# Convolution windows of three quarters with their own halo rows, and chunks that enter in pairs

## The chip, the cores and the metric

The kernel runs on one core of one Trainium2 chip. The metric is device time in microseconds, a median over runs. A profile of one execution gives the busy times of TensorE (PE), its weight loads (PEld), VectorE (DVE), ScalarE (ACT), GpSimd (POOL) and the DMA queues, among them SyncE's (SP).

## The reference

A causal convolution over 7 tokens, one softmaxed set of taps per head of 24 channels, is followed by a token mix over all 4224 tokens and a channel mix:

```python
w = softmax(weight, axis=-1)                   # 8 heads x 7 taps
x = conv(x, w)                                 # x: 8 x 4224 x 192, left padding of 6 zeros
theta = x @ w_theta
zr, zi = x * cos(theta), x * sin(theta)
y = w_tok_r @ zr + w_tok_i @ zi                # 4224 x 4224 each, over tokens
u = x + y
out = u + max(u @ w_ch, 0)
```

## The kernel before, in words

**Tiling.** Batch and channels lie side by side: a token is a row of 1536 values. The 4224 tokens that are summed over are cut into 33 *chunks* of 128 rows; a chunk is four *quarters* of 32 tokens that lie far apart (`tokens(c, a)`, line 158), so that 32x32 transposes can turn the token weights. The 4224 tokens that are put out are cut into 16 *units* of two 128-row tiles and one unit of a single tile. For a unit of two tiles a fast matrix product with seven products takes the place of eight; each product is done for two halves g of 384 columns. So a unit costs 14 matmuls of 384 columns per chunk (8 for the single tile).

**Chunks and visits.** At most `SLOTS` = 11 chunks lie in SBUF as operands (tiles r0, i0, r1, i1, t1, t2, t4). `FIRST` says in which visit of the first round each of the first 11 chunks enters; later chunks enter 17 visits after the chunk whose slot they take (lines 109 to 111). A *visit* is one unit against the chunks that are in: it loads its sums d from DRAM (L621), transposes the token weights (L507) and adds and subtracts them (L521), runs the products (L659), adds the results to d (L686 on DVE; the first of a unit's first visit are ACT copies, L684), and stores d (L698). L731 copies a partial product from bank x to bank y. In the first round visit v has v + 1 chunks, up to 11; there are 61 visits. A unit's last visit ends with the channel mix: ACT casts d (L780), a transpose by DMA or, in the last four visits, by TensorE (L438, copied by DVE in L443), the mix (L452), the final add (L799) and the store (L806).

**Preparing a chunk** (`Chunk.prepare`). POOL loads the four quarters of x with a cast (L224, 32 rows each). The tile xw holds two halves of 96 rows: two quarters with 16 halo rows each. The halo comes from the chunk before by a DMA from SBUF to SBUF on SP's queue (L265, four per chunk). Two matmuls per head accumulate the two halves (L403, 96 rows by 192 columns, 16 per chunk); the weights are banded matrices made at the start (L826 to L875). ACT copies two heads at a time to xz (L411, four per chunk). SP stores xz (L298) for the later residual. xz is transposed, by TensorE for the first 11 chunks and by DMA after, mixed with theta's weights (L452), clamped by DVE (L320), turned to sine and cosine by ACT (L348), multiplied (L357) and subtracted (L369). xw and xz have two buffers each.

**Order.** Every piece of work is a `Step` with an engine, a planned duration and what it must follow. `Schedule` plays the steps through a model of the engines, takes the ready step with the earliest due time, and emits the instructions in that order; a rehearsal sets the due times. Each engine then runs its instructions strictly in that order. Constants such as `LAND` (planned DMA times) and `START` (when each engine is through with the preamble) belong to this model. Banks 0 to 5 of PSUM hold the products (rows x, y, s for two g); only banks 6 and 7 serve convolution, transposes and mixes: a step with `mm` takes one, and the step with `frees` gives it back.

Of the kernel before, what the change touches and what calls it, by code (L numbers as in the profile page):

```python
# [16 lines left out]
def kernel(  # L17
# [22 lines left out]
    nc = tc.nc  # L40
# [9 lines left out]
    HALO = 16  # L50
    WR = Q + HALO
    NT = S // P
    HN = N // 2
# [4 lines left out]
    FIRST = (0, 1, 2, 3, 4, 5, 6, 7, 8, 9, 10)  # L58
    CLAMP = 1.5
    EXTRA = 3  # L60
    BY_PE = 4
    SMALL = 3
# [73 lines left out]
    def pair(u):  # L136
        return 2 * u + 1 < NT


    def pair(u):  # L140
        return 2 * u + 1 < NT


# [22 lines left out]
    class Step:  # L166
        def __init__(self, engine, us, run, after=(), lands=0.0, wire=0.0, frees=None, mm=False):
            self.engine, self.us, self.run = engine, us, run
            self.after, self.lands, self.wire = list(after), lands, wire
            self.frees, self.mm = frees, mm  # L170
            self.due, self.want, self.fixed, self.end = None, None, None, None
            self.number = len(steps)
            steps.append(self)

# [20 lines left out]

    bands = constp.tile([2 * WR, 2 * H + 1, 2, Q], BF16, name="bands")
    nc.vector.memset(bands, 0.0)


    def channel_weights(w, name, after=()):  # L200
        R = D - P
        made = {}

        def clear():
            made["t"] = t = wk.tile([P, 4, D], BF16, name=name, tag="wc", bufs=1)
            dve(nc.vector.memset(t[:, 1:3, :], 0.0))

        ready = [Step("dve", 0.25, clear, after)]
        for lo, hi, k, r0, r1 in ((0, P, 0, 0, P), (0, R, 1, P, D), (R, P, 2, 0, R), (0, P, 3, R, D)):
            ready.append(Step(  # L210
                "pool", 0.6, lambda lo=lo, hi=hi, k=k, r0=r0, r1=r1: pool(nc.gpsimd.dma_start(
                    out=made["t"][lo:hi, k, :], in_=w[r0:r1, :]
                )), ready[:1], lands=4.0, wire=0.3,
            ))
        return (lambda: made["t"]), ready

    xw = tiles(wk, 2, [2 * WR, 2, B, D], BF16, "xw")
    rings = {k: Ring(2) for k in ("xw", "xz", "uT", "ang", "xr", "st", "x", "y", "s")}
# [4 lines left out]
    def load_x(c, a, n, lo, t0, h, k):  # L223
        pool(nc.gpsimd.dma_start(  # L224
            out=xw[k][lo : lo + n, h, :, :],
            in_=x[:, t0 : t0 + n, :].rearrange("b s d -> s b d"),
        ))


    class Chunk:  # L230
        def __init__(self, c):
            self.c, self.early = c, c < SLOTS
            self.k, self.uses, prev = rings["xw"].take()
            self.loads = []
            for a in range(NQ):
                h, lo = a // 2, (a % 2) * WR
                t0 = tokens(c, a)
                if c or t0 == 0:
                    lo += HALO
                else:  # L240
                    t0 -= HALO
                n = (a % 2 + 1) * WR - lo
                args = (c, a, n, lo, t0, h, self.k)
                if c == 0:
                    if t0 == 0:
                        nc.vector.memset(xw[0][0:HALO, 0, :, :], 0.0)
                    load_x(*args)
                    s = Step("none", 0.0, None)
                    s.fixed = START["x0"]
                else:  # L250
                    s = Step(
                        "pool", 0.6, lambda args=args: load_x(*args), [prev],
                        lands=LAND["x"], wire=0.87,
                    )
                self.loads.append(s)
            self.uses += self.loads
            chunks[c] = self
            xwk = xw[self.k]
            self.filled = list(self.loads)
            if c:  # L260
                before = chunks[c - 1]

                def history(a):
                    h, lo = a // 2, (a % 2) * WR
                    sp(nc.sync.dma_start(  # L265
                        out=xwk[lo : lo + HALO, h, :, :],
                        in_=xw[before.k][lo + Q : lo + Q + HALO, h, :, :],
                    ))

                for a in range(NQ):  # L270
                    s = Step(
                        "sp", 0.6, lambda a=a: history(a), [before.loads, prev],
                        lands=LAND["history"], wire=0.15,
                    )
                    before.uses.append(s)
                    self.filled.append(s)
            self.uses += self.filled[NQ:]

        def prepare(self):
            c = self.c  # L280
            zk, self.xzuse, prev = rings["xz"].take()
            self.xz = xzt[zk]
            copies = []
            for hp in range(H // 2):
                m = Step("pe", 0.34, lambda b, hp=hp: self.conv(b, hp), [self.filled, bands_ready, prev], mm=True)
                self.uses.append(m)
                e = Step(
                    "act", 0.5, lambda b, hp=hp: self.conv_copy(b, hp), [m], frees=m
                )
                copies.append(e)  # L290
            self.xzuse += copies
            self.xf = self.xz[:, :, :].rearrange("p b d -> p (b d)")
            if c + 2 < NCH:
                Chunk(c + 2)
# [8 lines left out]
            for g in range(2):  # L303
# [3 lines left out]
                turned = transposed(src, uT, [copies, prev], self.early, "sp")  # L307
# [4 lines left out]
                for k2 in range(2):  # L312
# [3 lines left out]
                    )  # L316
                    uuse.append(m)
# [80 lines left out]
        def conv(self, b, hp):  # L398
            for hh in range(2):
                h = 2 * hp + hh  # L400
                for half in range(2):
                    at = 2 * h + 1 - half
                    pe(nc.tensor.matmul(  # L403
                        banks[b][:, hh * B * G : (hh + 1) * B * G],
                        lhsT=bands[:, at : at + 2, :, :].rearrange("p z a m -> p (z a m)"),
                        rhs=xw[self.k][:, half, :, h * G : (h + 1) * G],
                        start=(half == 0), stop=(half == 1),
                    ))

        def conv_copy(self, b, hp):  # L410
            act(nc.scalar.activation(  # L411
                out=self.xz[:, :, hp * 2 * G : (hp + 1) * 2 * G].rearrange(
                    "p b (h g) -> p h b g", h=2
                ),
                in_=banks[b][:, 0 : 2 * B * G].rearrange("p (h b g) -> p h b g", h=2, b=B),
                func=AT.Copy,
            ))

# [7 lines left out]
    def transposed(u, uT, after, by_pe, queue):  # L426
# [8 lines left out]
        def turn(b):  # L435
# [7 lines left out]
        e = Step("dve", 0.55, lambda b: dve(nc.vector.tensor_copy(  # L443
            out=got(uT).rearrange("p k s -> p (k s)"),
            in_=banks[b][:, :].bitcast(BF16)[:, 0 : 6 * P],
        )), [m], frees=m)
# [19 lines left out]
    class Weights:  # L466
# [89 lines left out]
        def tile(self, name):  # L556
            t = self.tiles[name]
            return small_tile()[:, t] if self.small else t
# [7 lines left out]
    def freed_xw():  # L566
        return [s for u in rings["xw"].uses[-2:] for s in u]


    def small_tile():  # L570
        big_tile()
        if "small" not in late:
            late["small"] = wk.tile([P, 7, SMALL, NQ, Q], BF16, name="small", tag="xw")
        return late["small"]

    def big_tile():
        if "big" not in late:
            late["big"] = wk.tile([P, 2, HN], F32, name="late", tag="xw")
        return late["big"]
# [5 lines left out]
    def container(k):  # L585
        if ("u", k) not in late:
            if k < 4:
                both = wk.tile([P, 2, HN], BF16, name="ubT", tag=("ang", "xz")[k % 2])
# [10 lines left out]
    class Visit:  # L599
# [79 lines left out]
        def add(self, q, bank, g, after, begins=False, ends=False):  # L679
            def run():  # L680
                o = self.d[q]()[:, g * PC : (g + 1) * PC]
                y = banks[bank][:, 0:PC]
                if self.first and begins:
                    act(nc.scalar.activation(out=o, in_=y, func=AT.Copy))  # L684
                else:
                    dve(nc.vector.tensor_tensor(out=o, in0=y, in1=o, op=ALU.add))  # L686

            if self.first and begins:
                s = Step("act", 0.49, run, [after, self.start[q]])
# [14 lines left out]
        def products(self):  # L704
# [4 lines left out]
            for r in "xys" if self.pair else "xy":  # L709
                for g in gs:  # L710
                    k, uses[r, g], prev[r, g] = rings[r].take()
                    rows[r, g] = 2 * "xys".index(r) + k

# [15 lines left out]
            def copy(g):  # L729
                kx, ky = rows["x", g], rows["y", g]  # L730
                s = Step("act", 0.48, lambda: act(nc.scalar.activation(  # L731
                    out=banks[ky][:, 0:PC], in_=banks[kx][:, 0:PC], func=AT.Copy
                )), [at["x", g], prev["y", g]])
# [39 lines left out]
        def output(self, q):  # L773
            k, use, prev = outring.take()
            if len(outring.uses) <= 5:
                prev = [
                    s for r in ("ang", "xz", "uT") for u in rings[r].uses[-2:] for s in u
# [37 lines left out]
    START = {"x0": 8.0, "pe": 12.3, "dve": 12.3, "act": 6.3, "pool": 6.6, "sp": 2.0}  # L815
    LAND = {
        "x": 9.0, "history": 6.0, "keep": 6.0, "turn": 11.0, "w": 8.0, "d": 7.5, "store": 5.5,
        "xr": 7.0, "out": 5.0,
    }
    EARLY, SLACK = {}, 12.0  # L820
    noise = wk.tile([P, 512], BF16, name="noise", tag="ang")
    nc.vector.memset(noise, 0.0)
    Chunk(0)
    masks = wk.tile([2 * WR, KS, 2, Q], BF16, name="masks", tag="ang")
# [240 lines left out]
```

## Time and profile before

| what | value |
|---|---|
| three runs | 1449.01, 1450.27, 1439.24 us; median 1449.01 |
| profiled execution | 1439.62 us, span 1437.5 us, mean granted clock 0.997 |
| PE busy | 1408.2 us, 98% of the span, 9486 matmuls |
| DVE / ACT / POOL busy | 1102.9 / 335.8 / 512.2 us |
| L659, products | 7656 matmuls (7572 from tile w, 84 from tile small) |
| L403, convolution | 528 matmuls |
| L411, copies of the convolution | 132, 489 ns each, on ACT |
| L224, loads of x | 132 |
| L265, halo copies by DMA | 128 |
| L443, copies of transposes | 38, 549 ns each, on DVE |

A line of the groups reads: line, engine, operation, output<-input, shape, count, then busy time and mean duration, then the idle time of the engine just before these instructions and what ended it. Matmuls overlap in the array, so that a matmul's duration is longer than its distance from the next.

### The profile page before, as it was taken

What the parts mean: (1) busy time and instruction counts of PE and PEld (TensorE: products, weight loads), DVE (VectorE), ACT (ScalarE), POOL (GpSimd) and SP (SyncE); (2) the same over time, 40 slices, a digit from 0 to 9 for tenths busy, and PEclk for the clock granted to TensorE, in tenths of its full rate; (3) what the DMA queues carried; (4) which work ended last, traced back from release to release, by engine and by line L of the source; (5) the groups of instructions that cost most, each with busy time, mean ns of one, the idle gap of its engine ahead of it and who ended that gap; (6) DMA issues with size and microseconds to landing.
All of it is one profiled execution on the core that took longest, in us unless ns stands there. A gap on an engine that the chain in (4) does not pass through costs nothing.

```text
span 1437.5 us, 24960 instructions
## 1 busy us (share of the span) xinstructions
PE 1408.2 (98%) x9486; PEld 895.5 (62%) x9486; DVE 1102.9 (77%) x1835; ACT 335.8 (23%) x582; POOL 512.2 (36%) x778
## 2 busy tenths in 40 slices
PE   6899999999999999999999999999999999999997
PEld 3666666666666666666666666666666666666665
DVE  7998764446778887886576788788887878787788
ACT  5764422122212212210000221122121212121221
POOL 7543321124234552133134445225553354311120
PEclk9999999999999999999999999999999999999999
DMA  9999883679999999998799999999995999999984
GB/s 140 252 220 209 155 162 94 122 131 238 202 222 239 237 225 229 225 210 198 183 195 193 234 252 234 220 224 217 250 253 124 204 279 257 220 229 208 254 209 154
DMA packets 341351, 298.44 MB, mean 208 GB/s; under 512 B 160784, under 2 KB 287760, under 8 KB 341232
## 3 DMA queue, kind: packets, MB, share of 16 engines
q0 software_dynamic: 171072, 97.81, 50.5%
q1 hardware_dynamic: 130160, 189.21, 42.6%
q10 hardware_dynamic: 40000, 9.84, 5.3%
q8 instruction: 74, 1.21, 0.4%
q14 instruction: 45, 0.37, 0.1%
HBM read 250.21 MB, written 106.56 MB: 248 GB/s over the span
## 4 chain that ended last, share of the span: by engine, by line
PE 90%; DMA 4%; DVE 2%; ACT 1%; issue 0%; ACTq 0%; DVEq 0%
PE bank L659 82%; PE bank L452 5%; DMA ubT<-ubT 3%; PE bank L403 3%; DMA out_dram<-d 1%; PE bank L438 1%; DVE d L799 0%; DVE d L686 0%; DVE w L521 0%; DMA xw<-xw 0%; DVE ubT L443 0%; ACT ubT L780 0%; DVE uT L443 0%; ACT bank L731 0%; DVE ang L320 0%
## 5 line engine op out<-in xcount | busy, mean ns | idle before, releaser
L659 PEld LDWEIGHTS <-w 128*128 128x128 bf16 x7572 | 736.7, 98 | 466.5 <-issue 5.1
L659 PE MATMUL bank<-t,w 128*128 128x384 bf16 x3198 | 558.4, 326 | 1.6 <-DVE w L521 1.4
L686 DVE TENSOR_TENSOR d<-bank,d 128x384 f32<-128x384 f32 x542 | 291.8, 548 | 186.0 <-PE bank L659 158.0
L659 PE MATMUL bank<-i,w 128*128 128x384 bf16 x2220 | 396.2, 326 | 1.2 <-ACT bank L731 0.6
L507 DVE STREAM_TRANSPOSE w<-st 128x640 bf16<-128x640 bf16 (+5 forms) x416 | 340.2, 846 | 67.0 <-PE bank L659 63.0
L659 PE MATMUL bank<-r,w 128*128 128x384 bf16 x2154 | 384.1, 326 | 1.4 <-DVE r L357 1.2
L485 POOL DMA_DIRECT2D st<-in_moe_w_tok_r_dram x244 | 140.2, 585 | 411.4 <-DVE w L507 354.5
L485 POOL DMA_DIRECT2D st<-in_moe_w_tok_i_dram x244 | 139.8, 583 | 145.8 <-DVE w L507 138.8
L521 DVE TENSOR_TENSOR w<-w 128x1408 bf16<-128x1408 bf16 (+10 forms) x220 | 183.2, 833 | 2.5
L631 POOL TENSOR_TENSOR d<-d,xr 128x768 f32<-128x768 f32 x62 | 105.6, 1704 | 142.1 <-DMA xr<-xs 91.8
L224 POOL DMA_DIRECT2D xw<-in_x_dram x132 | 76.8, 594 | 153.6 <-PE bank L403 128.0
L348 ACT ACTIVATE r<-ang,half_pi 128x768 bf16<-128x768 f32 x44 | 41.1, 933 | 310.3 <-DVE ang L320 310.3
L731 ACT ACTIVATE bank<-bank 128x384 f32<-128x384 f32 x116 | 54.8, 476 | 211.8 <-PE bank L659 196.7
L684 ACT ACTIVATE d<-bank 128x384 f32<-128x384 f32 x132 | 63.4, 491 | 160.4 <-PE bank L659 158.8
L411 ACT ACTIVATE xz<-bank 128x384 bf16<-128x384 f32 x132 | 60.5, 489 | 168.8 <-issue 115.4
L320 DVE TENSOR_SCALAR ang<-bank 128x384 f32<-128x384 f32 x132 | 68.5, 550 | 24.8 <-PE bank L452 24.4
L780 ACT ACTIVATE ubT<-d 128x768 bf16<-128x768 f32 x44 | 36.8, 842 | 147.1 <-DVE d L686 116.3
L799 DVE SCALAR_TENSOR_TENSOR d<-bank,d 128x384 f32<-128x384 f32 x106 | 55.3, 550 | 20.7 <-PE bank L452 20.1
L452 PEld LDWEIGHTS <-uT 128*128 128x128 bf16 x632 | 55.0, 98 | 17.0 <-issue 3.0
L403 PE MATMUL bank<-xw,bands 96*128 96x192 bf16 x528 | 60.6, 249 | 1.9 <-ACT xz L411 1.1
L452 PE MATMUL bank<-wth,uT 128*128 128x192 bf16 x528 | 58.0, 246 | 2.6 <-DVE ang L320 1.1
L403 PEld LDWEIGHTS <-bands 96*128 96x128 bf16 x528 | 47.4, 99 | 15.3 <-issue 4.0
(68 smaller groups left out, 546.3 us busy)
## 6 DMA issues: line engine op xcount, KB each, us to landing
part<-d SPq DMA_DIRECT2D x172, 384.0 KB, 4.2
d<-part SPq DMA_DIRECT2D x159, 384.0 KB, 5.5
st<-in_moe_w_tok_r_dram POOLq DMA_DIRECT2D x152, 176.0 KB, 6.5
st<-in_moe_w_tok_i_dram POOLq DMA_DIRECT2D x152, 176.0 KB, 7.4
out_dram<-d SPq DMA_DIRECT2D x53, 384.0 KB, 5.8
xs<-xz SPq DMA_DIRECT2D x132, 96.0 KB, 5.0
xr<-xs POOLq DMA_DIRECT2D x66, 192.0 KB, 6.4
xw<-in_x_dram POOLq DMA_DIRECT2D x129, 96.0 KB, 5.7
```

What stands on the lines that cost most here:

```text
L224: pool(nc.gpsimd.dma_start(out=xw[k][lo : lo + n, h, :, :], in_=x[:, t0 : t0 + n, :].rearrange("b s d -> s b d"),))
L320: "dve", 0.55, lambda b, k2=k2, g=g: dve(nc.vector.tensor_scalar(out=self.ang[g][:, k2 * 2 * D : (k2 + 1) * 2 * D], in0=banks[b][:, 0 : 2 ...
L403: pe(nc.tensor.matmul(banks[b][:, hh * B * G : (hh + 1) * B * G], lhsT=bands[:, at : at + 2, :, :].rearrange("p z a m -> p (z a m)"), rhs= ...
L411: act(nc.scalar.activation(out=self.xz[:, :, hp * 2 * G : (hp + 1) * 2 * G].rearrange("p b (h g) -> p h b g", h=2), in_=banks[b][:, 0 : 2 ...
L452: pe(nc.tensor.matmul(banks[bk][:, b * D : (b + 1) * D], lhsT=tT[:, 3 * k + b + i, :], rhs=w[:, 2 * b + i, :], start=(i == 0), stop=(i == ...
L485: "pool", 0.58, lambda a=a, t0=t0, i=i, w=w: pool(nc.gpsimd.dma_start(out=st[i][a * Q : (a + 1) * Q, 0:nb, 0 : n * Q], in_=w[r0 : r0 + nb ...
L507: lambda c=c, ce=ce: dve(nc.vector.transpose(self.tile(name)[:, c:ce, :, :], st[i][:, at : at + NQ, c * Q : ce * Q].rearrange("p bt (c j) ...
L521: s = Step("dve", 0.15 + 0.069 * n, lambda: dve(nc.vector.tensor_tensor(out=flat(self.tile(name)), in0=flat(self.tile(p)), in1=flat(self.t ...
L631: a = Step("pool", 1.75, lambda: pool(nc.gpsimd.tensor_tensor(out=tile_(), in0=tile_(), in1=xrt[k], op=ALU.add)), [r, s])
L659: pe(nc.tensor.matmul(banks[bank][:, 0:PC], lhsT=self.w.block(a, c), rhs=chunks[c].operand(b, g), start=(start and c == self.lo), stop=(c ...
L684: act(nc.scalar.activation(out=o, in_=y, func=AT.Copy))
L686: dve(nc.vector.tensor_tensor(out=o, in0=y, in1=o, op=ALU.add))
```

## The change

- `FIRST` becomes (0, 0, 1, 2, 3, 4, 5, 6, 7, 8, 8): the first two and the last two chunks of a round enter together. The first round starts with two chunks; chunks also enter in pairs at visits 17, 25, 34 and 42. There are 59 visits, and two small visits are moved forward in place of three.
- A *window* of three quarters takes the place of the chunk as the unit of the convolution: 3 x 38 = 114 rows, each quarter with its own 6 halo rows, loaded from DRAM. The halo copies on SP go away. One matmul per head and window does three quarters; 44 windows. The band tile has seven quarter blocks with the fourth zero, so that a slice of four blocks puts the three results on the right output rows, whichever quarter the window begins with.
- A window that spans two chunks, or begins with an odd quarter, needs two copies out of the bank: 28 copies per three chunks. `readers` counts them; the bank is free after the last.
- xw and xz have three buffers each; late tiles that reuse this space are cut to match.
- *Copies on either engine* (`copy_step`, `also`): the planner gives them to ACT or DVE, whichever takes them first: convolution copies of chunks under 4, first copies of a visit and bank copies in visits under 4, and all copies of TensorE's transposes. Other such copies stay on ACT.
- *Lent banks*: until the first visit's products need them, banks 2 to 5 serve the convolution of windows 0 and 1 and the transposes and mixes of chunk 0 (`lent`). The first visit's y rows begin with a matmul whose result is overwritten.
- The preamble makes the band tile in one product and three halving adds; warm-up matmuls are 24, not 18, and need only the zeroed noise tile; theta's weights and the first two windows are loaded by the preamble itself.

```diff
-    FIRST = (0, 1, 2, 3, 4, 5, 6, 7, 8, 9, 10)
+    FIRST = (0, 0, 1, 2, 3, 4, 5, 6, 7, 8, 8)
+    EITHER, TURNED = 4, 11
...
+    def copy_step(o, i, after, us, frees=None, either=False):
+        def run(*b):
+            if s.engine == "dve":
+                dve(nc.vector.tensor_copy(out=o(), in_=i(*b)))
+            else:
+                act(nc.scalar.activation(out=o(), in_=i(*b), func=AT.Copy))
+        s = Step("act", us, run, after, frees=frees)
+        s.also = "dve" if either else None
+        return s
...
-    bands = constp.tile([2 * WR, 2 * H + 1, 2, Q], BF16, name="bands")
-    nc.vector.memset(bands, 0.0)
+    bands = constp.tile([WR, H, NQ + WQ, Q], BF16, name="bands")
+    nc.vector.memset(bands[:, :, WQ, :], 0.0)
...
+    class Window:
+            for j in range(WQ):
+                c, a = divmod(self.m * WQ + j, NQ)
+                lo, t0, n = j * ROWS, tokens(c, a) - KS + 1, ROWS
...
+                def load(lo=lo, t0=t0, n=n):
+                    pool(nc.gpsimd.dma_start(
+                        out=xw[self.k][lo : lo + n, :, :],
+                        in_=x[:, t0 : t0 + n, :].rearrange("b s d -> s b d"),
+                    ))
+                if self.m < 2:
+                    load()
...
+                    s = Step("pool", 0.6, load, [prev], lands=LAND["x"], wire=1.0)
...
+            for c, quarters in into.items():
+                lo, hi = quarters[0], quarters[-1] + 1
+                if lo % 2 and hi - lo > 1:
+                    copies.append((c, lo, lo + 1))
+                    lo += 1
+                copies.append((c, lo, hi))
+            at = -a0 % NQ
+            def conv(b, hp):
+                for hh in range(2):
+                    h = 2 * hp + hh
+                    pe(nc.tensor.matmul(
+                        banks[b][:, hh * B * G : (hh + 1) * B * G],
+                        lhsT=bands[:, h, at : at + NQ, :].rearrange("p z m -> p (z m)"),
+                        rhs=xw[self.k][0:WR, :, h * G : (h + 1) * G],
+                        start=True, stop=True,
+                    ))
...
-                def history(a):
-                    h, lo = a // 2, (a % 2) * WR
-                    sp(nc.sync.dma_start(
-                        out=xwk[lo : lo + HALO, h, :, :],
-                        in_=xw[before.k][lo + Q : lo + Q + HALO, h, :, :],
-                    ))
...
-        e = Step("dve", 0.55, lambda b: dve(nc.vector.tensor_copy(
-            out=got(uT).rearrange("p k s -> p (k s)"),
-            in_=banks[b][:, :].bitcast(BF16)[:, 0 : 6 * P],
-        )), [m], frees=m)
+        e = copy_step(
+            lambda: got(uT).rearrange("p k s -> p (k s)"),
+            lambda b: banks[b][:, :].bitcast(BF16)[:, 0 : 6 * P], [m], 0.6, m, either=True,
+        )
...
+                        prev[r, g] = [s for s in steps if s.frees is not None and s.frees.lent]
+                        if r == "y":
+                            prev[r, g] = [Step(
+                                "pe", 0.17, lambda k=rows[r, g]: pe(nc.tensor.matmul(
+                                    banks[k][:, 0:PC], lhsT=ident,
+                                    rhs=wth()[:, 0:2, :].rearrange("p k d -> p (k d)"),
+                                    start=True, stop=True,
+                                )), [prev[r, g], wth_ready],
+                            )]
...
-    START = {"x0": 8.0, "pe": 12.3, "dve": 12.3, "act": 6.3, "pool": 6.6, "sp": 2.0}
+    START = {"x": (8.0, 11.0), "pe": 11.3, "dve": 11.3, "act": 6.3, "pool": 11.2, "sp": 2.0, "wth": 15.0}
...
+    terms = spool.tile([WR, KS, H, Q], BF16, name="terms", tag="st")
+    n = KS
+    while n > 1:
+        k = n // 2
         nc.vector.tensor_tensor(
+            out=terms[:, 0:k], in0=terms[:, 0:k], in1=terms[:, n - k : n], op=ALU.add
         )
+        n -= k
...
     for k in range(6):
-        for _ in range(3):
-            pe(nc.tensor.matmul(banks[k], lhsT=ident, rhs=noise, start=True, stop=True))
+        for _ in range(4):
+            pe(nc.tensor.matmul(banks[k], lhsT=noise[:, 0:P], rhs=noise, start=True, stop=True))
...
             if s.lands:
                 self.wire = max(self.wire, end + 1.0) + s.wire
-                end = max(end + s.lands, self.wire + 1.5)
+                end = max(end + s.lands * (0.5 if now < CALM else 1.0), self.wire + 1.5)
```

## The prediction

> **What bounds the kernel now.** I read the busy slices of the page first, then the table by stage, then the order of time of TensorE, then counted matmuls per stage.
>
> ```profile
> PE   6899999999999999999999999999999999999997
> DVE  7998764446778887886576788788887878787788
> ...
> PE 90%; DMA 4%; DVE 2%; ACT 1%; issue 0%; ACTq 0%; DVEq 0%
> ```
>
> TensorE is full except in the first two slices and the last, and the chain that ended last is TensorE for 90%. A busy TensorE can hide gaps, because a matmul's 326 ns overlap the next one's, so I price its work by starts:
>
> ```profile
> 334.31 0.82 PE L403 MATMUL bank<-xw,bands 96*128 96x192 bf16 x8
> 334.97 1.95 PE L659 MATMUL bank<-r,w 128*128 128x384 bf16 x11
> 336.76 3.74 PE L659 MATMUL bank<-t,w 128*128 128x384 bf16 x22
> 340.33 3.74 PE L659 MATMUL bank<-i,w 128*128 128x384 bf16 x22
> 343.91 3.74 PE L659 MATMUL bank<-t,w 128*128 128x384 bf16 x22
> ```
>
> 22 products take 3.575 us, 0.1625 us each; 8 convolution matmuls take 0.66, 0.0825 each. Nothing stands between the groups. Eight 128-row mix matmuls also advance TensorE by 0.66 (349.27 to 349.93 in the same view), so contraction rows do not set the price, columns do. Six transposes take 0.33, 0.055 each.
>
> All work: 7656 products x 0.1625 = 1244.1; 528 convolution, 528 + 528 mix matmuls x 0.0825 = 130.7; 228 transposes x 0.055 = 12.5; together 1387.3. Counted by stage (591 real matmuls before 100 us, 2292 after 1100) the span of 1437.5 splits into 12.2 before the first convolution + 1387.3 work + 18.7 lost by 100 + 1.7 lost up to 1100 + 13.2 lost up to the last matmul's end at 1433.1 + 4.4 of final adds and stores. So 1100 us in the middle are bound by TensorE with no slack; only the two ends have something else.
>
> ```profile
> 20.00:40.00 20.00, 17.10 (x103) 9.88 (x102) 17.51 (x39) 15.93 (x33) 10.69 (x19) 0.83 1.13 201
> 40.00:60.00 20.00, 18.01 (x148) 12.40 (x149) 19.57 (x43) 15.06 (x31) 12.25 (x23) 1.00 1.20 253
> ...
> 1400.00:1420.00 20.00, 19.77 (x158) 13.52 (x156) 17.60 (x38) 4.22 (x6) 0.00 (x0) 1.00 0.36 115
> 1420.00:1437.50 17.50, 10.31 (x98) 7.25 (x95) 12.80 (x26) 3.16 (x4) 0.00 (x0) 0.98 0.61 203
> ```
>
> Columns: stretch, length, PE, PEld, DVE, ACT, POOL, clock, DMA share, GB/s. At both ends DVE is the fullest engine besides TensorE (19.57 of 20 in the ramp), ACT is not (4.22 of 20 at the end).
>
> **The change, part by part** (span of the profiled execution; its time is 1439.62, 2.1 more).
>
> 1. *Convolution.* 44 windows x 8 = 352 matmuls in place of 528, each again 192 columns: 176 x 0.0825 = **-14.5**. It lies on TensorE in the stretch without slack (416 of the 528 run after 100 us), so nothing hides it and nothing else is late there: all next users find their operands ready now. A stall of 0.08 us per convolution step (176 steps) would undo it.
> 2. *Two seed matmuls* into the s or y banks: 2 x 0.1625 = +0.3. The six more warm-up matmuls end before the bands exist: 0; were they not covered, 6 x 0.3 = 1.9.
> 3. *Preamble.* POOL: three loads at 0.64 from 1.41, mask memset 0.74 and seven selects 0.31 (rows x 96/64) end at 6.2. DVE: two mask adds 0.43, one 1792-element product (256 take 0.42, so 2.0 at one element per 1.04 ns plus 0.15), three adds of 768, 512 and 256 (0.55, 0.41, 0.29), three scalings (0.38 each): bands at 11.6 in place of 12.14. But the second window's loads leave POOL only between 6.2 and 8.1; with the 4.0 to 5.7 us to landing that x loads show they land at 12.1 to 13.8, and chunk 0 needs its last quarter from them. The theta weights come earlier (issue ends at 11.7, not 15.2; TensorE waited 0.9 us for them), the first token-weight loads later (from 12.3, not 6.66), landing about when the first product could start (20.47 now). Value 0, from -1 to +1 while the loads land as now.
> 4. *Ramp.* An early chunk costs DVE 7.9 (4 clamps 0.55, 4 products 0.55, 4 differences 0.60, 2 copies 0.55); a first visit of n chunks 4 adds 2.2 + weights 1.3 + 0.78 n. TensorE: 3.3 a chunk now, 2.86 then, and 2.275 n a visit. Before, n = 1 to 5 with five chunks: DVE 68.7, TensorE 50.6, difference 18.1 (seen: 18.7). After, n = 2 to 5 with five chunks: 64.4 and 46.2, difference 18.2: entering in pairs alone gains nothing, as the work per visit shrinks on both engines. What can help is sharing. ACT does 51.9 there now (per chunk 5.5, per visit 4.9), 59.9 with 28 copies of 0.489 per three chunks in place of 12; shared evenly 62.2 each, difference 16.0. Bounds -2.1 and +4 (DVE, the fuller engine, taking eight copies of ACT's at 0.55); value **-1**.
> 5. *Two entering at once* at visits 17, 25, 34 and 42. Such a visit needs DVE 16.5 (12 adds 6.6, weights 9.9) + 2 x 7.2 = 30.9 and TensorE 25.0 + 4.4 = 29.4; at 42, with final adds, 35.3 against 32.1. The visits beside them leave DVE 3.5 us or more free (23.7 against 27.2), and the three x and xz buffers let preparation run ahead. Bounds 0 and 3 x 1.5 + 3.2 = 7.7; value **+1.5**, nearer the lower end since the present single entries cost only the 1.7.
> 6. *End.* After 1380 TensorE loses 6.2 while DVE is busy 48.8 of 57.5. 16 transpose copies x 0.55 = 8.8 may now go to ACT; half is 4.4. The closing visits (n = 4 last) stay. Bounds -5 and 0; value **-2**. The waits on DMA transposes stay, plus or minus 3:
>
> ```profile
> PE bank L452 <- DMA ubT<-ubT: 5.5, 4, 2.1
> ```
>
> 7. *Copies.* 308 convolution copies for 132: 86 us more on ACT, busy 336 of 1437.5, so hidden; but they lie in ACT's queue ahead of sines, bank copies and casts, and a bank of the two is held for two copies in 132 of the 176 steps. If that cover goes, up to 0.49 a step.
> 8. *Queues.* SP loses 128 history copies and 16 loads and stores of d (two visits fewer); none is on the chain: 0. POOL keeps its 132 x issues at 0.594, though of 38 rows: 0, and rival A otherwise.
>
> Sum: -14.5 + 0.3 + 0 - 1 + 1.5 - 2 = -15.7; span 1421.8, time 1423.9. The shown runs lie at 1449.01, 1450.27 and 1439.24, the profiled one at 1439.62: a mean of 1444.5, 4.9 above the profile. I add that: **1428.8**. Against the median of 1449.01, 1% is 14.5 us (a measurement of this kernel can tell about that from no change), so "faster" means under 1434.5.
>
> **A rule against the change.** No load of x here has a row count other than 32 or 48; 38 is new.
>
> ```profile
> q0 software_dynamic: 171072, 97.81, 50.5%
> ```
>
> A packet of this queue takes 0.505 x 16 x 1437.5 / 171072 = 0.068 us. A 38-row load has 304 rows of 768 bytes: over 16 engines 1.3 us, on one engine 20.7. I take the low end, the row of the 32- and 48-row loads being nearest. The Trainium skill, "DMA: Bandwidth & Descriptors", section "Why a DMA increments its semaphore by 16 and not by 1", says that a DMA uses the largest number of engines up to 16 that divides the slowest dimension, which would be 2 for 38 rows, but that on trn2 some direct copies from POOL's queue are spread over all by rounding up. By its first half a load would take an estimated 10.3 us and the sum would be that of rival A; by its exception it would stay my forecast.
>
> **Rivals.**
>
> A. *The 38-row loads use few engines.* Between 1.3 and 20.7 the middle is 11, 9 us more than now. Window 1 then lands near 22, chunk 0 is 9 us late, TensorE idles for that; later three buffers hide it. For: x loads already share queues that are never empty (DMA share 1.1 to 1.2). Against: nothing in this trace. 1428.8 + 9 = 1438: same.
>
> B. *The saving returns as waits of TensorE on DVE* at the four double entries (7.7 in place of 1.5) and the ramp gains nothing (+1): 1428.8 + 7.2 = 1436: same. For: DVE 30.9 against 29.4. Against: the gapless single entries.
>
> C. *ACT takes what DVE has too much of* at both ends: ramp -2.1, end -5, waits on DMA transposes -3: 7 less, 1422. For: ACT 4.22 of 20 at the end. Against: TensorE is nearly full up to 1420 there.
>
> D. *Banks.* Two copies in ACT's strict order hold a bank of the two; TensorE, in order too, stops at the next convolution or mix. Place: every convolution step from 100 us on. Half of the second copy uncovered is 0.245 x 176 = 43: 1472, slower. It decides "slower" from (1463.5 - 1428.8) / 176 = 0.20 us a step. Against: ACT is free 77% and products lie between the steps.
>
> **Chances.** Forecast 0.48, C 0.10, A 0.16, B 0.19, D 0.07. Faster 0.58 (forecast and C), same 0.35 (A and B), slower 0.07. The range goes from 1415 (C with the start's -1 and no run-to-run addition) to 1443 (A with a ramp of +4 more), leaving out D and the far ends.
>
> **What would show it.** 352 rows of the convolution line at 0.0825 a start, 8 in 0.66; the 1100 us in the middle still gapless, also near visit 17 (143 chunk products of 2.275 plus preparation and the ramp: some 385 us), 25, 34 and 42; no wait of TensorE on the copies of xz or on clamps; first convolution near 11.6 to 12.2 and first product near 20; work missing by 100 us between 16 and 19; copies to uT and ubT partly on ACT at the end; x landing near 5.7. Wrong if x lands in 10 or more, if TensorE's waits name the copies, or if the ends change by more than 8.

## The result, and the profile after

The changed kernel is **slower: 1583.34 us against 1444.59 us, medians of four runs each, ratio 1.096, 95% interval 1.091 to 1.102**. The forecast was 1428.8, the range ended at 1443. The profiled execution took 1582.66 us, its span is 1580.9.

From the page of the changed kernel: the busy slices of TensorE and DVE, the granted clock, the software queue, the chain that ended last by engine and by line, the loads of x on POOL, the convolution, and the time from issue to landing of a load of x.

```profile
PE   4678899999989989798999996997979999979998
...
DVE  5667775435576678566756775865769887666787
...
PEclk6899999999999999898999998998999999999999
...
q0 software_dynamic: 451392, 101.19, 61.9%
...
PE 50%; DMA 37%; POOL 5%; issue 4%; DVE 3%; SPq 1%; DVEq 0%; ACT 0%; POOLq 0%; ACTq 0%
PE bank L702 46%; DMA xw<-in_x_dram 18%; DMA st<-in_moe_w_tok_i_dram 5%; DMA st<-in_moe_w_tok_r_dram 5%; PE bank L490 3%; DMA xr<-xs 3%; POOL xw L267 2%; DMA uT<-xz 2%; DMA d<-part 1%; DMA part<-d 1%; DMA out_dram<-d 1%; DVE w L545 1%; POOL st L523 1%; POOL d L674 1%; DVE d L726 1%
...
L267 POOL DMA_DIRECT2D xw<-in_x_dram x132 | 189.3, 1440 | 98.9 <-PE bank L304 45.5
...
L304 PE MATMUL bank<-xw,bands 114*128 114x192 bf16 x352 | 54.3, 255 | 27.8 <-DMA xw<-in_x_dram 8.5
...
xw<-in_x_dram POOLq DMA_DIRECT2D x131, 114.0 KB, 14.8
```

The loads of x in the kernel before, on POOL and to their landing:

```profile
L224 POOL DMA_DIRECT2D xw<-in_x_dram x132 | 76.8, 594 | 153.6 <-PE bank L403 128.0
...
xw<-in_x_dram POOLq DMA_DIRECT2D x129, 96.0 KB, 5.7
```

TensorE is no longer full: of the slices that were nines, several now fall to 8 and 7 and one to 6, and the first four are the worst. The chain is TensorE for 50%, no longer 90%, and DMA for 37%. The row that changed most is a load of x: POOL needs 1440 ns to issue one, where it needed 594; it lands after 14.8 us, not 5.7; and the software queue, through which POOL's loads go, has 451392 packets (the pieces in which the profile records a transfer), not 171072, for nearly the same bytes (101.19 MB, before 97.81). The convolution itself came as forecast: 352 matmuls.

The table by stage of the changed kernel (stretch, length, PE, PEld, DVE, ACT, POOL, clock, DMA share, GB/s):

```profile
20.00:40.00 20.00, 9.75 (x61) 6.96 (x59) 11.29 (x25) 9.78 (x18) 15.28 (x15) 0.59 0.93 60
...
300.00:400.00 100.00, 100.00 (x617) 60.23 (x616) 46.79 (x60) 19.53 (x40) 21.58 (x39) 1.00 0.57 111
400.00:500.00 100.00, 92.86 (x616) 58.29 (x614) 68.46 (x109) 35.84 (x65) 42.90 (x45) 1.00 1.36 196
...
800.00:900.00 100.00, 100.00 (x626) 60.72 (x624) 63.26 (x93) 9.75 (x21) 30.39 (x41) 1.00 0.89 179
900.00:1000.00 100.00, 82.92 (x517) 51.57 (x516) 67.00 (x109) 25.51 (x43) 46.77 (x50) 0.90 1.24 189
```

From 300 to 400 and from 800 to 900 TensorE is full; from 400 to 500 and from 900 to 1000, where chunks enter, it idles 7 and 17 us. DVE, at 11.29 of 20 in the ramp, now idles itself. The clock falls with TensorE's idling (0.59 in the ramp, 0.90 from 900).

Who waited for whom (in total, times, longest):

```profile
POOL st L523 <- DMA xw<-in_x_dram: 175.3, 65, 6.5
...
DVE w L545 <- DMA st<-in_moe_w_tok_r_dram: 103.2, 14, 19.2
...
DVE w L545 <- DMA st<-in_moe_w_tok_i_dram: 69.7, 26, 11.3
...
PE bank L702 <- DVE d L726: 47.1, 16, 11.5
```

The first of these waits in the kernel before:

```profile
POOL st L485 <- DMA xw<-in_x_dram: 0.4, 1, 0.4
```

The wait spreads: POOL's next loads of token weights stand behind loads of x for 175 us (before 0.4; 2.0 with 39 rows, an experiment below), DVE's transposes of the weights wait for those, DVE works through its adds late, and TensorE waits for DVE. TensorE hardly waits for x itself (the convolution 8.5 us). Other transfers slow down as well: a 176 KB load of token weights lands after 9.8 us, not 6.5 or 7.4, a transposing DMA of xz after 11.0, not 6.7.

### The profile page after: what moved, and what is told of

Its sections match the earlier page's. It is cut to its first block, busy times and chain, and to the rows that moved or that the text cites. A ratio compares the mean times of both kernels' runs of the same rounds, so it can differ in the third digit from the quotient of the medians.

```text
span 1580.9 us, 24396 instructions
## 1 busy us (share of the span) xinstructions
PE 1434.5 (91%) x9318; PEld 898.2 (57%) x9318; DVE 1076.6 (68%) x1781; ACT 430.7 (27%) x761; POOL 616.7 (39%) x766
## 3 DMA queue, kind: packets, MB, share of 16 engines
q0 software_dynamic: 451392, 101.19, 61.9%
## 4 chain that ended last, share of the span: by engine, by line
PE 50%; DMA 37%; POOL 5%; issue 4%; DVE 3%; SPq 1%; DVEq 0%; ACT 0%; POOLq 0%; ACTq 0%
PE bank L702 46%; DMA xw<-in_x_dram 18%; DMA st<-in_moe_w_tok_i_dram 5%; DMA st<-in_moe_w_tok_r_dram 5%; PE bank L490 3%; DMA xr<-xs 3%; POOL xw L267 2%; DMA uT<-xz 2%; DMA d<-part 1%; DMA part<-d 1%; DMA out_dram<-d 1%; DVE w L545 1%; POOL st L523 1%; POOL d L674 1%; DVE d L726 1%
## 5 line engine op out<-in xcount | busy, mean ns | idle before, releaser
L702 PE MATMUL bank<-t,w 128*128 128x384 bf16 x3204 | 567.9, 328 | 11.0 <-DVE d L726 10.1
L545 DVE STREAM_TRANSPOSE w<-st 128x640 bf16<-128x640 bf16 (+4 forms) x412 | 342.9, 856 | 257.1 <-DMA st<-in_moe_w_tok_r_dram 103.2
L702 PE MATMUL bank<-r,w 128*128 128x384 bf16 x2158 | 404.5, 333 | 32.2 <-DVE d L726 16.9
L726 DVE TENSOR_TENSOR d<-bank,d 128x384 f32<-128x384 f32 x516 | 275.8, 543 | 155.1 <-PE bank L702 129.9
L267 POOL DMA_DIRECT2D xw<-in_x_dram x132 | 189.3, 1440 | 98.9 <-PE bank L304 45.5
L559 DVE TENSOR_TENSOR w<-w 128x1408 bf16<-128x1408 bf16 (+8 forms) x216 | 182.4, 844 | 2.3
L185 ACT ACTIVATE xz<-bank 32x384 bf16<-32x384 f32 (+2 forms) x299 | 139.9, 482 | 147.6 <-issue 84.0
L490 PE MATMUL bank<-wth,uT 128*128 128x192 bf16 x528 | 67.4, 269 | 34.6 <-DVE ang L378 20.2
L304 PE MATMUL bank<-xw,bands 114*128 114x192 bf16 x352 | 54.3, 255 | 27.8 <-DMA xw<-in_x_dram 8.5
L304 PEld LDWEIGHTS <-bands 114*128 114x128 bf16 x352 | 34.7, 101 | 47.7 <-issue 21.1
## 6 DMA issues: line engine op xcount, KB each, us to landing
xw<-in_x_dram POOLq DMA_DIRECT2D x131, 114.0 KB, 14.8
```

The lines of the kernel that those rows point to most:

```text
L185: act(nc.scalar.activation(out=o(), in_=i(*b), func=AT.Copy))
L267: pool(nc.gpsimd.dma_start(out=xw[self.k][lo : lo + n, :, :], in_=x[:, t0 : t0 + n, :].rearrange("b s d -> s b d"),))
L304: pe(nc.tensor.matmul(banks[b][:, hh * B * G : (hh + 1) * B * G], lhsT=bands[:, h, at : at + NQ, :].rearrange("p z m -> p (z m)"), rhs=xw[ ...
L490: pe(nc.tensor.matmul(banks[bk][:, b * D : (b + 1) * D], lhsT=tT[:, 3 * k + b + i, :], rhs=w[:, 2 * b + i, :], start=(i == 0), stop=(i == ...
L545: lambda c=c, ce=ce: dve(nc.vector.transpose(self.tile(name)[:, c:ce, :, :], st[i][:, at : at + NQ, c * Q : ce * Q].rearrange("p bt (c j) ...
L559: s = Step("dve", 0.15 + 0.069 * n, lambda: dve(nc.vector.tensor_tensor(out=flat(self.tile(name)), in0=flat(self.tile(p)), in1=flat(self.t ...
```

## Where the time went

TensorE's time, by the counting of the prediction (starts of 0.1625, 0.0825 and 0.055 us; the kernels named 48, 38 rows and so on are the experiments below):

| us | before | changed | before, 38 rows | changed, 42 rows |
|---|---|---|---|---|
| up to the first convolution | 12.2 | 14.6 | 12.5 | 11.6 |
| work | 1387.9 | 1373.8 | 1387.9 | 1373.8 |
| lost up to 220 us | 18.8 | 74.1 | 57.6 | 24.8 |
| lost from 220 to 1100 | 0 | 84.6 | 99.7 | 1.9 |
| lost from 1100 to the last matmul | 14.2 | 29.4 | 38.9 | 10.9 |
| after it | 4.4 | 4.4 | 4.5 | 4.5 |
| span | 1437.5 | 1580.9 | 1601.1 | 1427.5 |

The work is cut at 220 and 1100 us, and a matmul that crosses a cut counts on both sides, some 0.6 us in each column; time at a lower clock counts as lost. The convolution's saving is there in full (1387.9 to 1373.8, with the two seed matmuls). What was lost lies in the three rows of lost time: 188 us in the changed kernel, and 196 in the third column, which has the 38-row loads and neither windows nor pairs.

## The experiments

**1. The row count alone, in the kernel before.** First each quarter is loaded with its own 16 halo rows, without the copies on SP:

```diff
-                if c or t0 == 0:
-                    lo += HALO
-                else:
-                    t0 -= HALO
-                n = (a % 2 + 1) * WR - lo
+                own = HALO if t0 else 0
+                lo += HALO - own
+                t0 -= own
+                n = Q + own
...
-                def history(a):
...
```

> The kernel before, with each quarter of x loaded with its own 16 halo rows (48 rows, 384 packets) and without the halo copies on SP. Theory R (row count): 38 is no multiple of 16, so its loads are cut into 8 times as many packets; 48 is one, so packets of the load line stay at 8 a row, landing near 6 us, time as before, 1440 to 1450. Rival H (the extra halo bytes of x cost, whatever the row count): 1.5 times the bytes of a 32-row load, more than the 38-row loads' 1.19 times, so clearly slower, over 1500. Rival W (the windows, pairs and copies cost, not the loads): as before.

Measured: 1447.46, ratio 1.0044 (1.0021 to 1.0067); 187456 packets, POOL 627 ns an issue (median), landing 6.5 us.

Then the same kernel with 6 halo rows from chunk 2 on (`own = HALO if c < 2 else KS - 1`), so that 124 loads have 38 rows:

> As the 48-row kernel, but from chunk 2 on each quarter is loaded with 6 halo rows (38 rows); nothing else of the change. Theory R: POOL needs about 1.44 us to issue such a load, in place of 0.59, packets of the software queue rise by some 270 thousand, landing is 10 us or more, and the time rises by 60 to 150 us over the 48-row kernel. Rival H: under the 48-row kernel. Rival W: as the 48-row kernel, within 1%.

Measured: **1602.82, ratio 1.1098 (1.1019 to 1.1178)**. From its page, the queue, the loads on POOL and their landing:

```profile
q0 software_dynamic: 441408, 101.35, 60.0%
...
L224 POOL DMA_DIRECT2D xw<-in_x_dram x132 | 183.7, 1402 | 69.5 <-PE bank L384 45.0
...
xw<-in_x_dram POOLq DMA_DIRECT2D x124, 114.0 KB, 13.5
```

Fewer bytes, 155 us more (expected were 60 to 150). Neither windows nor pairs nor copies are in this kernel, so rivals H and W of the expectations fall.

**2. Other row counts in the changed kernel.** First 40 rows, 8 of halo, with the bands moved to match:

```diff
-    ROWS = Q + KS - 1
+    PAD = 8
+    ROWS = Q + PAD
...
-                lo, t0, n = j * ROWS, tokens(c, a) - KS + 1, ROWS
+                lo, t0, n = j * ROWS, tokens(c, a) - PAD, ROWS
```

> The changed kernel with 8 halo rows in place of 6, so that a quarter is loaded as 40 rows and a window has 120. Theory R: 40 is a multiple of 8, so a load has 640 packets in place of 2432, landing 5 to 9 us, and most of the 140 us go: 1425 to 1450. Rival W: as the changed kernel, 1570 to 1590. Rival H: a little slower than the changed kernel, 1585 to 1600.

Measured: **1437.93, ratio 0.9947 (0.9910 to 0.9985)**; 145 us came back for two rows more per load. 199872 packets, POOL 722 ns, landing 5.6 us.

With the 38 rows loaded as 32 and 6 (`cuts = [(lo, t0, n - Q), (lo + n - Q, t0 + n - Q, Q)]`):

> The changed kernel with each 38-row load cut into one of 32 rows and one of 6 rows. Theory R: 256 + 384 = 640 packets a quarter, as with 40 rows, but twice as many loads to issue (264 at some 0.6 us): 1430 to 1470. Rival W: 1570 to 1600. Rival H: as the changed kernel.

Measured: 1435.87, ratio 0.9964 (0.9933 to 0.9995). So far the theory of rows cut into pieces held in its times, but not in its packets: 512 a load with 40 rows and 400 for 32 and 6, not 640. It was put to a row count for which it foretells the opposite of its neighbours, 42 (`PAD = 10`):

> The changed kernel with 10 halo rows, so that a quarter is loaded as 42 rows: more rows than the 40 that ran at 1438, less than the 48 that ran at 1447 in the kernel before. Theory R (a load's rows are cut into 16 / gcd(rows, 16) pieces): 42 = 2 x 21, so 8 pieces a row, 42 x 8 x 8 = 2688 packets a load, some 490 thousand packets on the software queue, POOL 1.4 to 1.6 us an issue, time 1570 to 1620. Rival (the 40 rows are fast because a window fills more of the 128 partitions, or for any reason that is smooth in the row count): 1430 to 1460.

Measured: 1429.18 in one run, POOL 676 ns, 183104 packets. **The theory of pieces fell.** The packets tell which rule fits instead: 131 of the 132 loads have the full rows, and if a load counts 16 x 8 x rows / k packets, k being the largest number up to 16 that divides the rows, then 42 gives k = 14 and 384, 40 gives 10 and 512, 38 gives 2 and 2432. Taking 131 of these from each queue's total leaves 132800 in all three kernels. Two more counts, one row to either side, tell it from anything smooth. 39 rows:

> The changed kernel with 7 halo rows, 39 rows a load: one more than 38. The theory of pieces fell with 42 rows (24 packets an engine, not 168). Theory K (a load uses the largest number of engines up to 16 that divides its rows, and every engine of the queue is charged the same): 39 = 3 x 13, 13 engines, 3 rows each, 384 packets, POOL under 0.7 us, landing 5 to 7 us, 1425 to 1445. Rival S (from 39 rows down to 38 nothing special happens; what helps at 40 and 42 is the fuller window): 1500 to 1590.

Measured: 1437.09, ratio 0.9956 (0.9925 to 0.9988). The same three lines of its page:

```profile
q0 software_dynamic: 183104, 100.51, 52.6%
...
L268 POOL DMA_DIRECT2D xw<-in_x_dram x132 | 88.3, 676 | 179.8 <-PE bank L305 113.2
...
xw<-in_x_dram POOLq DMA_DIRECT2D x131, 117.0 KB, 5.3
```

41 rows:

> The changed kernel with 9 halo rows, 41 rows a load. Theory K: 41 is prime, one engine, 41 x 8 x 16 = 5248 packets a load, some 820 thousand on the software queue, POOL over 2 us an issue, landing over 25 us, and clearly slower than with 38 rows: 1700 or more. Rival S: 1425 to 1445, as with 40 and 42.

Measured: **2028.11** in one run. The same three lines:

```profile
q0 software_dynamic: 820288, 103.86, 59.9%
...
L268 POOL DMA_DIRECT2D xw<-in_x_dram x132 | 329.0, 2496 | 323.4 <-issue 250.7
...
xw<-in_x_dram POOLq DMA_DIRECT2D x131, 123.0 KB, 20.1
```

The totals again leave 132800, to the packet, with k = 13 and k = 1. In the kernel before the same rule leaves 136896 for 32, 38 and 48 rows. What these packets are, their sizes tell. From the pages of the changed kernel and of the one with 39 rows:

```profile
DMA packets 615269, 289.20 MB, mean 183 GB/s; under 512 B 438800, under 2 KB 565776, under 8 KB 615152
...
DMA packets 346981, 288.53 MB, mean 201 GB/s; under 512 B 170512, under 2 KB 297488, under 8 KB 346864
```

They differ by 268288 packets under 512 bytes, which is 2048 for each of 131 loads, just what the rule gives (2432 less 384). In the packed traces the software queue has 11104 packets of 4 bytes in the kernel before, 16 for each of its 694 issues; 20280 with 39 rows, 289616 with 38 and 655368 with 41. So of the 2432 packets of a 38-row load 304 carry data, 8 of 384 bytes for each row, and 2128 are of 4 bytes: as if each of 16 engines got as many packets as the two with data. The 16 small packets that every issue has besides are also why a 6-row load of the split kernel counts 144, where the rule gives 128. The traces do not name the engines, but while any packet of 384 bytes is on its way, there are on average 4.7 of them with 38 rows and 2.6 with 41, against 11.8 with 39 and 11.1 in the kernel before.

POOL's time to issue follows the packets of one engine, a sixteenth of the load's: 584 ns for 16 (medians), 627 for 24 (676 in the windows), 722 for 32, 1441 for 152, 2505 for 328. In landing, expected over 25 us, the 41 rows gave only 20.1; that POOL's slow issuing spaces the loads would explain it, but is not shown.

**3. Is it only that the loads are asked for too late?** The planner is told 1.44 us of POOL, a landing of 20 us and 4 us of wire for each 38-row load:

```diff
-                    s = Step("pool", 0.6, load, [prev], lands=LAND["x"], wire=1.0)
+                    s = Step("pool", 1.44, load, [prev], lands=LAND["x"], wire=4.0)
...
-        "x": 9.0, "keep": 6.0,
+        "x": 20.0, "keep": 6.0,
...
-                end = max(end + s.lands * (0.5 if now < CALM else 1.0), self.wire + 1.5)
+                end = max(end + s.lands, self.wire + 1.5)
```

> The changed kernel, 38 rows as they are, but the planner is told that a load of x takes POOL 1.44 us, lands 20 us after it and fills the wire for 4. If the loss is loads that are merely asked for too late: back to 1440 to 1480. If the packets themselves hold up the other transfers and POOL: still over 1550.

Measured: 1711.97, ratio 1.186 (1.179 to 1.193), landing 13.0. A plan with these numbers didn't bring it back; it made it worse. That no plan could is not shown by one. Which part of such a load does the harm, POOL's longer issuing, the many packets of 4 bytes or the data on few engines, stays open: in every run here the three come together.

**4. With the loads mended, where is the other half of the forecast gain?** The 42-row kernel was timed again:

> The kernel with 42 rows again, timed: 1428 to 1440, ratio 0.990 to 0.997. By the counts of its profile it has the convolution's saving in full (14), but loses 25 by 220 us where the kernel before loses 19.

Measured: **1435.24, ratio 0.9947 (0.9917 to 0.9977)**, the profiled execution 1426.27. Its gain over the kernel before is 7.5, where 15.7 was forecast, and it is faster than both kernels of this study (than the kernel before by 0.2 to 0.8%). From its table by stage (the execution of 1429.18; columns as above):

```profile
20.00:40.00 20.00, 15.00 (x91) 8.70 (x90) 17.15 (x38) 15.24 (x29) 12.37 (x20) 0.81 1.05 128
40.00:60.00 20.00, 17.12 (x123) 10.41 (x121) 19.41 (x43) 18.01 (x34) 11.16 (x20) 1.00 1.24 219
...
600.00:800.00 200.00, 200.00 (x1244) 121.23 (x1243) 134.59 (x204) 13.53 (x26) 56.97 (x85) 1.00 0.87 193
```

From 600 to 800 TensorE is full, as it is from 100 to 400 and from 800 to 1000. The ramp is worse than before: 24.6 us lost by 100 us (100 - 11.6 - 63.8 of work), before 18.7. ACT has 18.01 of 20 from 40 to 60, before 15.06. Parts of the change were undone or varied in turn.

Single entries (`FIRST = (0, 1, 2, ..., 10)`), with 40 rows:

> The 40-row kernel with one chunk entering per visit as in the kernel before (FIRST from 0 to 10), all else as in it. If entering in pairs costs what I gave it (+1.5 and -1 of ramp): the same as 1438 within 5. If the double entries eat the convolution's saving: 1425 to 1432. If pairs help the ramp: 1442 to 1450.

Measured: 1439.92, ratio 0.9948 (0.9912 to 0.9984); lost by 100 us 26.6, against 25.6 with pairs and 40 rows. Pairs are worth 1 in the ramp and nothing that the time can tell.

Copies on their old engines, with 40 rows (`EITHER = 0`, the copy of `transposed` on DVE):

> The 40-row kernel with all copies on the engine that had them before (convolution, first copies and bank copies on ACT, transposes on DVE). By my terms sharing was worth 1 in the ramp and 2 at the end: 1441 against 1438. If sharing is what carries the ramp with two chunks in it: 1445 to 1455. If DVE takes copies that it has no time for: 1430 to 1436.

Measured: 1435.82, ratio 0.9962 (0.9935 to 0.9988); lost by 100 us 26.7, so sharing is worth 1.1 there, and the times don't part. Sharing further, up to chunk 11 (`EITHER = 11`), with 42 rows:

> The 42-row kernel with copies on either engine for chunks and visits up to 11, not 4. If the ramp's loss is ACT's (18.0 of 20 us busy from 40 to 60, 16.7 from 60 to 80, with 28 copies per three chunks in place of 12): 2 to 5 under the 42-row kernel. If DVE (19.4 of 20) is what is short: the same or up to 5 above.

Measured: 1435.61, ratio 0.9961 (0.9932 to 0.9990); lost by 100 us 28.1, more than the 24.6 without. That fits DVE having no time for them (19.41 of 20 us busy from 40 to 60 without).

Theta's weights loaded by the planner:

```diff
-    wth, wth_ready = channel_weights(moe_w_theta, "wth")
+    wth, wth_ready = channel_weights(moe_w_theta, "wth", [])
```

(and `START["pool"]` 9.2, not 11.2.)

> The 42-row kernel with theta's weights loaded by the planner, as in the kernel before, not by the preamble ahead of the first token weights. If those late weights (first S1 product at 24.1 us) are the ramp's loss: time lost by 100 us falls from 24 to 20 or 21 and the time by 3. If not: 24 as it is, time the same within 1.

Measured: 1434.09, ratio 0.9935 (0.9905 to 0.9965), the lowest median of the kernels timed more than once, but within the interval of the 42 rows; lost by 100 us 24.9. Not the cause.

No lent banks and no seed matmuls:

> The 42-row kernel with banks 6 and 7 alone for convolution, transposes and mixes, no seed matmuls. If lending helps at all, more than 24 lost by 100 us (25 to 27), if its waits cost, 21 to 23.

Measured: 1430.46 in one run, lost by 100 us 24.9. Lending is worth nothing that this one run can tell.

The windows and the new preamble without the rest: single entries, old engines, no lent banks, 42 rows:

> The 42-row kernel with single entries, copies on the engines of the kernel before, no lent banks: windows of three quarters and the new preamble alone. If the windows cost the ramp (28 copies per three chunks, two windows for a chunk): 26 to 29 lost by 100 us. If it is the pairs, lending or sharing: 19 to 21.

Measured: 1445.96 in one run; lost by 100 us **33.1**, more than the 26 to 29 expected.

```profile
20.00:40.00 20.00, 11.60 (x68) 6.69 (x67) 14.38 (x36) 12.02 (x24) 14.13 (x24) 0.82 1.29 195
40.00:60.00 20.00, 15.14 (x105) 9.16 (x105) 17.39 (x37) 17.84 (x37) 8.56 (x14) 1.00 0.93 164
```

In the fence, columns as above, neither DVE nor TensorE is full up to 60 us, and the first product comes at 23.76, before at 20.47. So the windows of three quarters, with the new preamble that comes with them, cost the ramp 14 us against the kernel before (33.1 against 18.7; one run), and pairs, lending and sharing together win back 8 to 9 of it, more than any one of them alone. That the windows do it and not the preamble, and that chunks come late because a chunk needs two windows and its copies share ACT with the neighbour's, is argued from the counts and was not tested by itself.

## Why the prediction was wrong

**The step that failed is part 8, "POOL keeps its 132 x issues at 0.594, though of 38 rows: 0".** Measured: 1.440 us an issue and 14.8 us to landing. The 0.594 was kept without a row that shows 38, and for the transfer the low end of 1.3 to 20.7 us was taken, because a row of 32 or 48 rows was the nearest it had for 38, as if the price ran smoothly with the size; it doesn't, 39 and 41 rows lie 590 us apart. The 155 us that the row count alone costs the kernel before cover the whole loss (139) and the gain that the mended kernels show (7).

**Rival A named the mechanism and got its landing right**: the middle of its bounds was 11, "9 us more than now", and the landing rose by 9.1. That the middle of bounds sixteenfold apart hit so well is partly luck: with 41 rows, one engine by the same rule, its sum gives 328 x 0.068 = 22.3 us, 21 more than now, and the landing rose by 14.4. The Trainium skill's rule ("DMA: Bandwidth & Descriptors", "Why a DMA increments its semaphore by 16 and not by 1") gives 2 engines for 38 rows, 1 for 41, 13 for 39. The packets agree in every one of these, 152, 328 and 24 to an engine, POOL's times follow them, and its exception for POOL's queue did not apply here: rounded up to three rows an engine, 38 and 41 rows would have 24 packets as well. What failed in the rival is its reach, 1438 in place of 1583: "chunk 0 is 9 us late ... later three buffers hide it". Buffers hide a late x; they do not hide what the loads do to POOL's queue and to every other transfer. 74.1 us were lost by 220, not 28, and 84.6 from 220 to 1100, not 0. Its chance of 0.16 was too small as well: against it the prediction named nothing in the trace.

Point by point:

- *The split of the time before*: the 1.7 lost up to 1100 is not there. The 2292 matmuls after 1100 count six twice, at the cuts between four stretches; counted whole, TensorE loses 0 from 100 to 1100 and 14.2 after, not 13.2. The forecast hardly rests on it.
- *Convolution, -14.5*: right, 176 matmuls fewer, each still 0.0825 (4 in 0.33 us with 42 rows). In the mended kernels it is there; with pairs, the middle loses 1.7 to 3.7 in place of 0.
- *Preamble, 0*: with 42 rows the first convolution comes 0.6 earlier (11.58; worked out: 11.6) and the first product at 20.1, before 20.47. Right, as long as the loads land. In the changed kernel the two late windows put it 7 later (27.29).
- *Ramp, -1*: wrong in size even with mended loads, +5.9. The sum weighed only DVE's and ACT's work and took the ramp for bound by it; the windows with the new preamble cost 14 with neither DVE nor ACT full up to 60 us (17.39 and 17.84 of 20 at most), and the other parts win back 8 to 9. Pairs and sharing, priced at -1 together, gave about that each.
- *Pairs, +1.5*: about right. From 220 to 1100 the mended kernels with pairs lose 1.7 to 3.7, the two with single entries 0.1 and 0.6; the times don't part.
- *End, -2*: not settled. From 1100 on, executions of mended kernels lost between 6.9 and 27 us, the profiled one of before 14.2, and that spread is wider than the term.
- *Copies on ACT hidden; banks (rival D)*: right as far as the waits show, the convolution waits for copies of xz 2.3 us in all of the changed kernel, not 43.
- *Range*: its upper end took rival A's price at its first chunk only.

## What to carry to other kernels

A DMA's cost can jump with one row: before the row count of a load like these (POOL's queue, with a cast) changes, find its largest divisor up to 16, and pad to a count that has a large one (39 or 42 here, not 38 or 41), even though that moves more bytes. A slow load on a shared queue costs far beyond the buffer that it fills; price what stands behind it on the same queue, and read the wait of the issuing engine, not only that of the consumer. And where no row of the trace shows a new shape, the range must reach to the far bound over every use of it, not over the first.

## What was not expected of the hardware

- A load of x with 41 rows made POOL issue for 2496 ns, and with 39 rows for 676 ns.
- The packets that the profile counts for a load are 16 times the share of one engine, if k is the number of engines: 2432 for k = 2 and 384 for k = 13, for nearly the same bytes. What goes beyond the data, 2128 packets of the 38-row load and 72 of the 39-row load, has 4 bytes a packet.
- One mended kernel runs between 1426 and 1445 us (42 rows), another between 1430 and 1447 (40 rows). In the profiles at 1426.27 and 1447.45 the difference of the loss after 1100 us, 6.9 and 27, makes up nearly all of it. Why was not looked into.
